# The opening of a Mamba-2 SSD and gated feed-forward kernel: x issued behind B, the first weights fetched by halves, and the masks and fillers moved

## The chip, the cores and the metric

The kernel runs on one core of a Trainium2 chip. The metric is the device time of one execution in microseconds. A core has TensorE (PE for its products, PEld for its weight loads), VectorE (DVE), ScalarE (ACT), GpSimd (POOL) and SyncE (SP); transfers are issued on the queues of SyncE, ScalarE and GpSimd.

## What is computed

A chunked state-space scan (SSD) with 4 batches, 8 heads, 768 positions, head size 32 and state size 16; its result, turned to 3072 tokens of 256 features, goes through a feed-forward with a quick GELU.

```python
def _attn_ref(x, a, B, C):
    log_a = np.log(np.clip(a, 1e-06, 1.0))
    for c in range(nc):                      # chunks of 32 positions
        cum = np.cumsum(la, axis=-1)
        L = np.exp(cum[:, :, :, None] - cum[:, :, None, :]) * causal
        M = np.einsum('bhin,bhjn->bhij', Cc, Bc) * L
        y_intra = np.einsum('bhij,bhjd->bhid', M, xc)
        y_inter = np.einsum('bhin,bhnd->bhid', Cc, state) * np.exp(cum)[:, :, :, None]
        y[:, :, sl] = y_intra + y_inter
        Bx = np.einsum('bhjn,bhjd->bhjnd', Bc, xc) * decay_from_j[:, :, :, None, None]
        state = decay_full[:, :, None, None] * state + np.sum(Bx, axis=2)

def _moe_ref(x, w_in, w_out):                # 3072 x 256, 256 x 2048, 2048 x 256
    h = x @ w_in
    g = h * (1.0 / (1.0 + np.exp(-1.702 * h)))
    return g @ w_out
```

`w_in` and `w_out` arrive as 64-bit floats; the kernel reads them as pairs of 32-bit words and makes fp32 of them on the chip.

## The kernel before

The tokens go in six groups of 512 (`g`): 128 positions of each of the 4 batches. Each group has two pairs (`p`) of batches. For each group the SSD makes `yT`, the feed-forward's input; `hidden` and `project_all` (group 0) or the steps of `first` and `product` (the later groups) are the dense work. Each engine executes its instructions in the order in which the program text emits them: `in_order` at the end ties each instruction to the one before it on its engine. So the place of a call in the text is its place in the engine's queue, and a wait holds all that is behind it on that engine.

The change lies in the opening, the SSD of group 0 before the first dense product, and in its surroundings:

- **Loads.** `a` goes out first on SyncE. C's eight blocks are issued alternately by ScalarE and SyncE, B's eight by GpSimd (five) and SyncE (three), both by `load_blocks` (L130). Behind B, SyncE issues `fetch(0)`, the first piece of w_in, in two transfers (L179). GpSimd makes `pick` and `first`, then issues x of pair 0 (`load`, L146, two transfers); x of pair 1 stands further down, behind `drop_of(0)`.
- **Decays.** ScalarE takes the logarithm of a (L364), VectorE's scan (L368) makes `cum`. On PE, `mask` (L506) and `differ` (L512) make the exponents of both pairs in PSUM, `rows_first` (L501) those of the states; ScalarE's `decay_exp` (L542) makes `L`. Ahead of them PE runs fillers that compute nothing of use: `pads` (L427, 32 x 32 products) and `dense` (L431, wide ones).
- **Scores.** `turn_blocks` (L554) transposes C and B on VectorE. The masked copies of C are made for pair 0 by VectorE (`mask_first`, L578) and for pair 1 by ScalarE (`mask_blocks`, L587). `score` (L610) multiplies, and `weigh` (L621) multiplies the scores into `L` in place. `turn_back` (L568) transposes B back, `ends_first` (L473) scales it.
- **y and state.** `finish` step 0 has `intra` (L735) of pair 0, `gain` (L641) makes the increment of the state out of x and the scaled B, `keep_first` (L657) copies it on ScalarE, `finish` step 1 has `intra` of pair 1, `inter` (L722) and the four copies to `yT` (L747).
- **Weights.** A piece of w_in goes through `fields` (L200, L203), `clamp` (L212, L214, on ScalarE), `rounded` (L219) and `join` (L233, L239). Pieces 0 to 3 hold two of the sixteen column blocks `f` each, pieces 4 and 5 four each. `hidden(0, f)` (L796) needs block `f`, and `narrow` continues the pieces between the `hidden` calls.
- **Tables.** `table(f)` (L313) is a tiny activation that makes ScalarE switch to the function's table: Ln, then Exp, then Silu.
- `fold_ident(k)` (L350) makes two halves of `idents`, which the scans of later pairs read. `held` in `fetch` is a one-column memset on an engine, which makes the transfer wait for that engine's place.

Of the kernel before, what the change touches and what calls it, by code (L numbers as in the profile page):

```python
# [8 lines left out]
FP32 = mybir.dt.float32  # L9
# [26 lines left out]
def kernel(  # L36
# [122 lines left out]
    def fetch(i, queue=nc.sync, held=None):  # L159
        name, f, n = PIECES[i]  # L160
        if n == 2 and f % 4:
            t = pieces.pop(i - 1)[:, 2 * n * DM:]
        else:
            t = pieces[i] = words(f"bits{i}")
            t = t[:, :2 * n * DM]
        if held:
            held.memset(t[:, :1], 0)
# [7 lines left out]
        for k in range(2):  # L175
            if i:
                queue.dma_start(out=dst[k], in_=src[k])
            else:
                queue.dma_start(out=dst[:, :, k].rearrange("k p e -> p k e"),  # L179
                                in_=src[:, :, k].rearrange("k p e -> p k e"))  # L180
# [116 lines left out]
    fetch(0)  # L297
    pick = const.tile([P, NB, Q], FP32, name="pick")
    nc.gpsimd.memset(pick, 1.0)
    for r in range(R):  # L300
        rows = pick[32 * r:32 * r + 32]
        nc.gpsimd.affine_select(out=rows, in_=rows, pattern=[[-NH, NB], [-1, Q]],  # L302
                                compare_op=ALU.is_equal, fill=0.0, base=-Q * r,
                                channel_multiplier=1)
    firsts[0] = ssd.tile([P, NB, P], FP32, tag="first", name="first", bufs=1)
    nc.gpsimd.memset(firsts[0], 0.0)
    load(0, "x", nc.gpsimd)
# [55 lines left out]
    for k in range(2):  # L363
# [5 lines left out]
        out=flat_cum, data0=carry, data1=flat_cum, initial=0.0, op0=ALU.mult, op1=ALU.add)  # L369

# [317 lines left out]
    def finish(pairs, steps=range(2)):  # L688
# [56 lines left out]
        if early:  # L745
# [5 lines left out]
            if 0 in steps:  # L751
                for k in range(2):
                    dense(begun_y["banks"][0][:, 2 * P:])
                intra(0, pairs[0])
                return
            for t in range(NK):
                intra(1, pairs[1], (t,))
                copied(0, t)
# [28 lines left out]
    def hidden(g, f):  # L787
# [4 lines left out]
        for k in range(NK):  # L792
            n = 1 if g or NK * f + k < 5 else 4 if NK * (NF - f) - k <= 12 else 2
# [268 lines left out]
    pads(14, busy)  # L1062
    dense(busy, 3)
# [8 lines left out]
    pads(16, both[:, 0, 2 * P:], False)  # L1072
    differ_of(0)
    turn_blocks(0, "C")
    mask_blocks(1)
    decay_exp(0, None, both[:, :, :2 * Q * H])
    drop_of(0)
    load(1, "x", nc.gpsimd)
    mask_first(0)
# [4 lines left out]
    table(AF.Silu)  # L1084
# [3 lines left out]
    turn_blocks(0, "B")  # L1088
    score(range(PG))
    turn_back()  # L1090
    fold_ident(1)
# [3 lines left out]
    fetch(1, held=nc.vector)  # L1095
    weigh(0, (slice(1, 2),))
    fields(0, (0,), 1)
# [16 lines left out]
    finish(range(PG), (1,))  # L1114
    join(0, 2, (0,))
# [5 lines left out]
    rounded(1)  # L1121
    join(1, 2, (0,))
# [236 lines left out]
```

## Time and profile before

| | |
|---|---|
| median of 3 runs | 349.73 us (348.93 to 352.75) |
| the profiled execution | 349.18 us, of which the span is 347.5 us |
| PE busy | 341.1 us, 98% of the span |
| PEld, VectorE, ScalarE, GpSimd busy | 281.0, 256.2, 150.0, 46.0 us |
| granted TensorE clock (mean) | 1.00 |
| first dense product of group 0 (L796) starts | 17.26 us |
| last of x's transfers for group 0 lands | 14.46 us |

The span runs from the program's first instruction to its last; the 1.68 us around it belong to the execution's time. All times within the profile are counted from the span's start. A row of the timeline gives start, length, engine, line, operation, output and inputs; the bracket is the idle time of that engine ahead of the row and what ended it. "issue" there is idle time for which the profile shows no cause.

### The profile page before, as it was taken

The page shows a single profiled execution, that of the slowest core. Times are in us where ns is not written, and L with a number is a line of the kernel's source. Part 1 is how long each engine was busy: PE and PEld are TensorE (multiplying, and loading weights), DVE is VectorE, ACT ScalarE, POOL GpSimd, SP SyncE. Part 2 cuts the span into 40 slices and gives each one's busy share as a digit, 9 for nine tenths or more (in the row PEclk, how much of TensorE's full clock was granted, in tenths as well). Part 3 has the DMA queues.
Part 4 walks back from the last instruction along what each step waited for, and adds up shares of the span by engine and source line. Part 5 has one row for each costly group of instructions (what it writes and reads, how often), then busy time and mean ns, then how long its engine had stood idle before and what let it go on. Part 6 is the DMA issues. An engine that isn't in the chain of part 4 may idle for free.

```text
span 347.5 us, 8538 instructions
## 1 busy us (share of the span) xinstructions
PE 341.1 (98%) x3514; PEld 281.0 (81%) x3514; DVE 256.2 (74%) x477; ACT 150.0 (43%) x335; POOL 46.0 (13%) x82
## 2 busy tenths in 40 slices
PE   8799999999999999999999999999999999999996
PEld 6668964555788888888888888888888888899996
DVE  7889999999799897839985639985555653555463
ACT  6779664005454314644333543442444322554320
POOL 8305820300495000000000000000000000000000
PEclk9999999999999999999999999999999999999999
DMA  4699995704639000554122345120000120000221
GB/s 129 208 298 281 279 165 125 116 24 76 106 85 135 2 0 17 89 116 89 29 35 61 47 100 100 25 33 6 2 4 0 20 32 12 0 2 0 33 31 60
DMA packets 82831, 25.79 MB, mean 74 GB/s; under 512 B 68856, under 2 KB 81144, under 8 KB 82792
## 3 DMA queue, kind: packets, MB, share of 16 engines
q1 hardware_dynamic: 79912, 23.19, 31.4%
q0 software_dynamic: 1888, 1.74, 2.4%
q8 instruction: 27, 0.44, 0.5%
q10 hardware_dynamic: 992, 0.33, 0.4%
q14 instruction: 12, 0.10, 0.1%
HBM read 21.99 MB, written 3.24 MB: 73 GB/s over the span
## 4 chain that ended last, share of the span: by engine, by line
PE 95%; POOL 2%; DMA 1%; issue 0%; ACT 0%; DVE 0%; POOLq 0%
PE acc L954 28%; PE X L852 19%; PE Y L862 14%; PE h L796 10%; PE o L894 8%; PE acc L961 7%; PE y L735 2%; PE y L722 2%; PE cb L610 2%; PE A L641 1%; DMA x<-in_x_dram 1%; POOL zB L130 1%; POOL x L146 1%; POOL pick L302 0%; ACT S L657 0%
## 5 line engine op out<-in xcount | busy, mean ns | idle before, releaser
L857 ACT ACTIVATE ac<-X 128x256 f32<-128x256 f32 x76 | 29.1, 383 | 79.8 <-PE X L852 79.4
L954 PE MATMUL acc<-mg,mw 128*128 128x256 f32 x192 | 54.5, 379 | 0.0
L981 DVE TENSOR_TENSOR gT<-Y,ac 128x512 f32<-128x512 f32 x38 | 26.2, 690 | 37.1 <-PE Y L862 33.6
L829 ACT ACTIVATE gT<-gT 128x512 f32<-128x512 f32 (+1 forms) x76 | 39.3, 519 | 31.6 <-DVE gT L981 31.0
L852 PE MATMUL X<-my,mi 128*128 128x256 f32 x152 | 45.1, 379 | 0.0
L981 DVE TENSOR_TENSOR gT<-Y,b 128x256 f32<-128x256 f32 x38 | 15.8, 418 | 34.4 <-PE Y L862 34.4
L954 PEld LDWEIGHTS acc<-mg,mw 128*128 128x128 f32 x192 | 36.5, 190 | 5.0
L796 PE MATMUL h<-yT,w_in 128*128 128x128 f32 (+2 forms) x182 | 36.3, 357 | 0.1
L954 PE MATMUL acc<-gT,w_out 128*128 128x256 f32 x128 | 35.5, 379 | 0.0
L796 PEld LDWEIGHTS h<-yT,w_in 128*128 128x128 f32 x182 | 26.8, 191 | 8.3 <-issue 5.6
L852 PEld LDWEIGHTS X<-my,mi 128*128 128x128 f32 x152 | 28.0, 190 | 3.7
L894 PE MATMUL o<-gT,w_out 128*128 128x512 f32 x64 | 28.6, 597 | 0.0
L820 DVE TENSOR_TENSOR mg<-gT 128x512 f32<-128x512 f32 x40 | 27.2, 681 | 0.0
L954 PEld LDWEIGHTS acc<-gT,w_out 128*128 128x128 f32 x128 | 24.2, 190 | 3.4 <-ACT yT L769 0.2
L857 ACT ACTIVATE b<-X 128x256 f32<-128x256 f32 x38 | 14.6, 384 | 20.6 <-PE X L852 20.2
L852 PE MATMUL X<-yT,w_in 128*128 128x256 f32 x76 | 23.2, 389 | 0.0
L862 PE MATMUL Y<-yT,w_in 128*128 128x256 f32 x76 | 22.7, 381 | 0.0
L862 PE MATMUL Y<-my,mi 128*128 128x256 f32 x76 | 22.6, 379 | 0.0
L852 PE MATMUL X<-my,w_in 128*128 128x256 f32 x76 | 22.6, 381 | 0.0
L862 PE MATMUL Y<-yT,mi 128*128 128x256 f32 x76 | 22.5, 379 | 0.0
L894 PEld LDWEIGHTS o<-gT,w_out 128*128 128x128 f32 x64 | 11.8, 190 | 13.2 <-issue 12.4
L1013 POOL DMA_DIRECT2D out_dram<-ob x32 | 17.4, 551 | 26.5 <-DVE ob L1008 26.1
(144 smaller groups left out, 578.9 us busy)
## 6 DMA issues: line engine op xcount, KB each, us to landing
a<-scratch SPq DMA_DIRECT2D x18, 256.0 KB
bits<-in_moe_w_out_dram SPq DMA_DIRECT2D x8, 512.0 KB
x<-in_x_dram SPq DMA_DIRECT2D x20, 128.0 KB
bits<-in_moe_w_in_dram SPq DMA_DIRECT2D x8, 256.0 KB
bits<-in_moe_w_in_dram SPq DMA_DIRECT2D x4, 512.0 KB
out_dram<-ob SPq DMA_DIRECT2D x128, 16.0 KB
af<-in_a_dram SPq DMA_DIRECT2D x20, 64.0 KB
zC<-in_C_dram SPq DMA_DIRECT2D x36, 32.0 KB
```

The source lines that it names most:

```text
L610: nc.tensor.matmul(out=s["cb"][side, r, k].rearrange("p (q i) -> p q i", q=Q), lhsT=BT[rows, k, side], rhs=CT[rows, k, :, side], start=Tru ...
L796: nc.tensor.matmul(out=h[:, cols], lhsT=w_in[:, f, k], rhs=yT[g][:, k, cols], start=(k == 0 and e == 0), stop=(k == NK - 1), skip_group_ch ...
L820: nc.vector.tensor_tensor(out=t[:, 0:2], in0=B[:, :, 1], in1=B[:, 0], op=ALU.subtract)
L829: nc.scalar.activation(o, i, AF.Silu, scale=GELU_SCALE)
L852: nc.tensor.matmul(out=s["X"], lhsT=lhsT, rhs=rhs, start=i == "1", stop=i == "4", skip_group_check=True)
L857: nc.scalar.activation(copy, s["X"], AF.Copy)
L862: nc.tensor.matmul(out=o, lhsT=lhsT, rhs=rhs, start=s.pop("new", False), stop=i != "5", skip_group_check=True)
L894: nc.tensor.matmul(out=o[c], lhsT=w_out[:, c, f], rhs=gT[g, f // 2][:, f % 2], start=(f == 0), stop=(f == NF - 1), skip_group_check=True)
L954: nc.tensor.matmul(out=acc[g][0][i], lhsT=w, rhs=h, start=(j == 0 and (i, 0) in begins), stop=(j == NF // 2 - 1), skip_group_check=True)
L961: nc.tensor.matmul(out=o[k] if type(o) is list else o[:, cols], lhsT=h[:, cols], rhs=w, start=(j == 0 and (i, k) in begins), stop=(j == NF ...
L981: nc.vector.tensor_tensor(out=o, in0=v, in1=w, op=ALU.add)
L1013: (nc.sync if g else nc.gpsimd).dma_start(out=rows[:, b, :, cols], in_=t[32 * r:32 * r + 32, b * P:(b + 1) * P].rearrange("p (u e) -> p u ...
```

## The change

- x of both pairs is issued by GpSimd directly behind B; `pick` and `first` are made later, behind `since_start`.
- `fetch(0)` is split into its two halves (one column block each), held by VectorE: the first behind the scan of `cum`, the second behind C's turn.
- B is turned directly behind C. ScalarE masks C of pair 0, VectorE that of pair 1.
- The switch to the Silu table moves from behind the second exponentials to behind the copies of `finish` step 1.
- `fold_ident(1)` moves from behind `turn_back` to behind `rounded(1)`; the first field operation of piece 0's second half moves between the two `weigh` products of pair 0.
- Fillers: 14 `pads` ahead of the masks become one more `dense`; 16 `pads` ahead of `differ` become 27; one of the two `dense` in `finish` step 0 moves behind the first part of `intra` in step 1. One more product of `hidden(0, 9)` is cut into four instead of two.

```diff
--- before.py
+++ after.py
@@ -156,15 +156,18 @@
     def words(name):
         return wide.tile([P, 2 * PN], U32, tag="bits", name=name, bufs=BUFS)
 
-    def fetch(i, queue=nc.sync, held=None):
+    def fetch(i, queue=nc.sync, held=None, halves=range(2)):
         name, f, n = PIECES[i]
-        if n == 2 and f % 4:
+        if i in pieces:
+            t = pieces[i][:, :2 * n * DM]
+        elif n == 2 and f % 4:
             t = pieces.pop(i - 1)[:, 2 * n * DM:]
         else:
             t = pieces[i] = words(f"bits{i}")
             t = t[:, :2 * n * DM]
         if held:
-            held.memset(t[:, :1], 0)
+            at = 0 if i else 2 * halves[0] * DM
+            held.memset(t[:, at:at + 1], 0)
         if name == "in":
             src = moe_w_in[:, 2 * f * P:2 * (f + n) * P].rearrange("(k p) e -> p k e", p=P)
             dst, src = (v.rearrange(s, h=n, e=2 * P) for v, s in (
@@ -172,7 +175,7 @@
         else:
             src = moe_w_out[f * P:(f + n) * P, :].rearrange("(f p) (h e) -> h p f e", p=P, h=2)
             dst = t.rearrange("p (h f e) -> h p f e", h=2, f=n)
-        for k in range(2):
+        for k in halves:
             if i:
                 queue.dma_start(out=dst[k], in_=src[k])
             else:
@@ -294,17 +297,8 @@
                                 compare_op=ALU.is_ge, fill=-1e5, base=0,
                                 channel_multiplier=-1)
     load_blocks(0, "B", [nc.gpsimd, nc.sync, nc.gpsimd, nc.sync, nc.gpsimd, nc.sync, nc.gpsimd, nc.gpsimd])
-    fetch(0)
-    pick = const.tile([P, NB, Q], FP32, name="pick")
-    nc.gpsimd.memset(pick, 1.0)
-    for r in range(R):
-        rows = pick[32 * r:32 * r + 32]
-        nc.gpsimd.affine_select(out=rows, in_=rows, pattern=[[-NH, NB], [-1, Q]],
-                                compare_op=ALU.is_equal, fill=0.0, base=-Q * r,
-                                channel_multiplier=1)
-    firsts[0] = ssd.tile([P, NB, P], FP32, tag="first", name="first", bufs=1)
-    nc.gpsimd.memset(firsts[0], 0.0)
-    load(0, "x", nc.gpsimd)
+    for p in range(PG):
+        load(p, "x", nc.gpsimd)
     early = const.tile([P, 1], FP32, name="early")
     nc.vector.memset(early, 1.0)
 
@@ -367,6 +361,7 @@
     flat_cum = cum.rearrange("p k s -> p (k s)")
     nc.vector.tensor_tensor_scan(
         out=flat_cum, data0=carry, data1=flat_cum, initial=0.0, op0=ALU.mult, op1=ALU.add)
+    fetch(0, held=nc.vector, halves=(0,))
 
     fans, flat = {}, {}
 
@@ -749,12 +744,13 @@
                     AF.Copy)
 
             if 0 in steps:
-                for k in range(2):
-                    dense(begun_y["banks"][0][:, 2 * P:])
+                dense(begun_y["banks"][0][:, 2 * P:])
                 intra(0, pairs[0])
                 return
             for t in range(NK):
                 intra(1, pairs[1], (t,))
+                if t == 0:
+                    dense(begun_y["banks"][0][:, 2 * P:])
                 copied(0, t)
                 for n, p in enumerate(pairs):
                     inter(n, p, (t,))
@@ -790,7 +786,7 @@
             block(g, j)
         h = bank(f"h{g}_{f}")
         for k in range(NK):
-            n = 1 if g or NK * f + k < 5 else 4 if NK * (NF - f) - k <= 12 else 2
+            n = 1 if g or NK * f + k < 5 else 4 if NK * (NF - f) - k <= 13 else 2
             for e in range(n):
                 cols = slice(e * TG // n, (e + 1) * TG // n)
                 nc.tensor.matmul(out=h[:, cols], lhsT=w_in[:, f, k], rhs=yT[g][:, k, cols],
@@ -1059,8 +1055,8 @@
         differ(p, [(r, ab[p, r]) for r in range(R)])
 
     busy = bank("busy")
-    pads(14, busy)
-    dense(busy, 3)
+    for k in range(2):
+        dense(busy, 3)
     both = area("ab0")
     for r in range(R):
         mask_banks(0, r, both[:, r])
@@ -1069,32 +1065,39 @@
         mask_banks(1, r, seconds[r])
     for r in range(3):
         dense(both[:, r, 2 * P:], 3, False)
-    pads(16, both[:, 0, 2 * P:], False)
+    pads(27, both[:, 0, 2 * P:], False)
     differ_of(0)
     turn_blocks(0, "C")
-    mask_blocks(1)
+    fetch(0, held=nc.vector, halves=(1,))
+    turn_blocks(0, "B")
+    mask_blocks(0)
     decay_exp(0, None, both[:, :, :2 * Q * H])
     drop_of(0)
-    load(1, "x", nc.gpsimd)
-    mask_first(0)
+    mask_first(1)
     differ_of(1)
     rows_first(seconds)
     for r in range(R):
         decay_exp(1, r, seconds[r][:, :3 * P])
-    table(AF.Silu)
     drop_of(1)
     for p in range(PG):
         since_start(p, nc.gpsimd)
-    turn_blocks(0, "B")
+    pick = const.tile([P, NB, Q], FP32, name="pick")
+    nc.gpsimd.memset(pick, 1.0)
+    for r in range(R):
+        rows = pick[32 * r:32 * r + 32]
+        nc.gpsimd.affine_select(out=rows, in_=rows, pattern=[[-NH, NB], [-1, Q]],
+                                compare_op=ALU.is_equal, fill=0.0, base=-Q * r,
+                                channel_multiplier=1)
+    firsts[0] = ssd.tile([P, NB, P], FP32, tag="first", name="first", bufs=1)
+    nc.gpsimd.memset(firsts[0], 0.0)
     score(range(PG))
     turn_back()
-    fold_ident(1)
     fields(0, half=0)
     clamp(0, half=0)
     weigh(0, (slice(0, 1),))
     fetch(1, held=nc.vector)
+    fields(0, (0,), 1)
     weigh(0, (slice(1, 2),))
-    fields(0, (0,), 1)
     clamp(0, half=1)
     for i in range(2, 6):
         fetch(i, held=nc.vector if i == 2 else None)
@@ -1112,6 +1115,7 @@
     gain(range(PG), (0,))
     keep_first(0)
     finish(range(PG), (1,))
+    table(AF.Silu)
     join(0, 2, (0,))
     fields(0, (1,), 1)
     rounded(0, 1)
@@ -1119,6 +1123,7 @@
     fields(1)
     clamp(1)
     rounded(1)
+    fold_ident(1)
     join(1, 2, (0,))
     fields(2)
     clamp(2)
```

## The prediction

> **What bounds the kernel now.** First the page: PE is busy 341.1 of 347.5 us and carries 95% of the chain that ended last, so nearly all that an edit can win lies where PE idles. The busy times by stage put that before 17.3 us (PE busy 3.93 of 5 us in 10:15, 4.50 in 15:20, 5.00 from 20 on, 4.94 in 30:35). So the second view is the chain of waits in order of time:
>
> ```profile
> 7.23 1.77 POOL x L146 x2
> 8.99 0.04 issue
> 9.04 0.27 POOL drops L467
> 9.31 0.85 POOL x L146
> 10.15 4.30 DMA x<-in_x_dram
> 14.46 0.04 issue
> 14.50 0.36 PE y L641 x8
> ...
> 32.09 0.06 issue
> ```
>
> Columns: start, length, what. Ahead of these rows the chain runs on GpSimd through B's issues, `pick` (from 5.14) and `first` (to 7.23); then GpSimd issues x; the last of x's four transfers lands at 14.46; the state increment (L641), its copy (L657, from 14.88), y (L722) and, from 17.33, the dense stage (L796) follow. The last row is the one stop of the dense stage. But the chain names only who was last. Third, the timeline of each engine, for who is second:
>
> ```profile
> 10.28 0.41 PEld L610 LDWEIGHTS cb<-CT,Bt 32*64 32x64 f32 x21 [0.73 <-issue]
> ...
> 11.05 1.29 DVE L621 TENSOR_TENSOR L<-L,cb 128x512 f32<-128x512 f32 x2 [1.39 <-PE cb L610]
> ...
> 10.48 1.28 ACT L313 ACT_TABLE_LOAD   x1
> ...
> 19.16 0.43 DVE L233 SCALAR_TENSOR_TENSOR p<-bits,p 128x256 uint32<-128x256 uint32 x1 [0.75 <-ACT p L214]
> ...
> 25.09 0.69 DVE L200 TENSOR_SCALAR p<-bits 128x1024 uint32<-128x1024 uint32 x1 [0.26 <-DMA bits<-in_moe_w_in_dram]
> ...
> 30.81 1.19 DVE L239 SCALAR_TENSOR_TENSOR w_in<-m,p 128x512 f32<-128x512 f32 x1
> ...
> 32.12 0.94 PEld L796 LDWEIGHTS h<-yT,w_in 128*128 128x128 f32 x5 [0.43 <-ACT p L214]
> ```
>
> Start, length, engine, line, instruction, and in brackets the idle time ahead of it. Three readings. The x wait is only 0.43 us deep on the weight loads of L641. Before it, VectorE waited 1.39 us for the scores, which had stopped 0.73 us inside for nothing that the profile shows. And the last three rows are a second chain, VectorE making w_in out of 64-bit words: it has 0.75 + 0.26 us of slack between 11 and 32 us, and at 32.1 PE waits for it. The row names ScalarE, but the clamp there ended at 31.88; what ended last is w_in, at 30.81 + 1.19 = 32.00. So an earlier start of the dense stage is kept only if the weights come earlier too.
>
> **The change, part by part.**
>
> (a) x straight behind B. Out of x's way go `pick`, `first` (5.14 to 7.23) and `drops` (0.27). The last B issue ends at 5.10, four x issues of 0.90 follow, the last from 7.80. Landing takes 3.1 to 4.3 us (the rows of x), so 10.9 to 12.1. The reader comes to it at about 14.1. The wait goes: 0.43 us. The GpSimd work moved back is wanted first at 32.7 (`X<-az,pick`), and GpSimd idled from 12.1 to 28.9: nothing, and up to 2.1 us of its own time without that cover.
>
> (b) First weights by halves. The SyncE issues move from 5.16 and 5.64 to behind the scan (about 5.97) and behind C's turn (about 7.05). They landed 2.9 and 3.1 us after issue, the last sixteenth of the second 4.7. So 8.9, and 9.9 to 11.7. The first is read at 9.0, under VectorE's wait for the scores: nothing. The second is read between the two `weigh` products at about 11.3: 0 to 0.4, I take 0. Nothing stands behind them on SyncE until the fetch of piece 1. The two memsets are 0.06 each.
>
> (c) B turned behind C, masks swapped. The C mask of 0.69 leaves the place ahead of B's turn. B's transfers are complete only at 7.20 to 7.40 (semaphore updates), with weight packets among them from 6.7; without those perhaps 6.9. The turn starts at 7.1 to 7.3 instead of 7.59, and pair 1's mask ends at about 8.9. But the scores also wait for ScalarE's first exponential (ended 8.75) and PE's own `rows_first` (8.80), against 8.73 for B's turn. Alone this is worth nothing.
>
> (d) PE's fillers. Ahead of the masks 28 small products are swapped for two wide ones (+0.1 us), ahead of `differ` come 54 small ones instead of 32. The 32 took 0.27, so 54 take 0.46. `differ` starts at about 6.2 instead of 5.95, and so do `rows_first`, the second exponentials and the scores: -0.05 to +0.25 late, I take 0.22.
>
> (e) The stop of 0.73 in the scores. The DMA view of 7.8:7.9 has
>
> ```profile
> q1 hardware_dynamic: 31, 0.03, 79.9%
> q8 instruction: 1, 0.02, 59.2%
> ```
>
> one 16 KB instruction packet among the weight packets (948 ns, ended 8.78, 1.5 us before PE went on). The page counts 27 such packets for PE's 7028 rows, one for each 260, so they are taken as PE's own blocks of instructions. If the stop is that packet's lateness, its request at about 6.2 had a crowded 1.6 us; with the weights 0.8 and 1.4 us later it starts around 7.2 and most of the stop goes. Bounds 0 and 0.73; I take 0.57, since the place fits. The Trainium skill (Runtime: NRT & Kernel Launch, Instruction fetch mechanics) has it that the next 16 KiB block is fetched while the present one runs and that crossing is mostly hidden; the trace shows a stop that is not hidden. By the rule the stop has another cause and stays, and the forecast would be 350.1.
>
> (d) and (e) give the scores 0.35 earlier. `weigh`, `ends_first` and the second `weigh` keep their lengths and move by that; the field operation put between the first two only changes places with one behind them.
>
> (f) The second wide filler goes behind part of `intra`: two rows of some 0.25 in the 0.50 that PE waits for S; 0 to 0.1, taken as 0. One more product of f = 9 is cut into four: the stretch of fours takes 10.92/12 = 0.91 us for each 512 columns, the one of twos 5.38/6 = 0.90: nothing.
>
> So the last copy of y ends 0.43 + 0.35 = 0.78 earlier: 16.98 instead of 17.76.
>
> (g) The switch to Silu. Before, it ran from 10.48 to 11.88 with its first use, and ScalarE later idled 1.03 ahead of L657: free. After, it stands behind the last copy and ahead of the clamp of piece 1 (17.66), which had no slack at all: VectorE's 0.75 wait was for it. 1.40 - 0.78 = 0.62 later. The other idents product (0.67) moves into that wait, which is now 1.4 long: nothing, 0.67 without it. From there VectorE is full to 32.0 but for the 0.26 wait on a transfer, whose issue moves 0.35 earlier; I let it take up the 0.26. So w_in for f = 8 comes 0.62 - 0.26 = 0.36 later. PE, 0.78 early, stops some 0.65 at f = 2 and the rest at f = 8, and is 0.36 late. After that it never idles in the windows to 60.
>
> The skill (ScalarE: Activation LUTs, What ACT_TABLE_LOAD costs) adds a drain of 1.38 us to every switch's 1.28. The rows disagree: exponential ended 10.46, load 10.48, next activation 11.77. With it the sum would be 350.9.
>
> **Sum.** The profiled execution took 349.18 (span 347.5 and 1.68 around it); + 0.36 gives 349.5, 0.2 under the median 349.73 of runs that spread from 348.93 to 352.75. A measurement tells about 1% (3.5 us) from no change here, so I forecast no change.
>
> **Rivals.**
>
> Weights keep pace (faster). The stop goes whole and the fillers are free: copies 0.43 + 0.73 = 1.16 earlier, clamp 0.24 late, less 0.26: level. And w_in at 30.81 took 1.19 where its equals take 0.69, while GpSimd clipped `az` from 30.57; if they no longer meet, 0.5 more: 348.7. For: the packet's time. Against: the clip waits for a transfer that moves along.
>
> x is not early enough. x, both weight halves and an instruction packet now share the engines from 7.5 to 11; the last sixteenth of x came 1.3 us behind the other fifteen before. If it still comes at 14.4 the 0.43 is lost: 349.9. Against: two us to spare.
>
> The instruction block (slower). PE enters its next block near 9.9 instead of 10.3 and needs the one behind it at about 13.9. The packet for it started at 12.34; the one after that only at 19.70, 5.1 us after its place was reached at 14.6, when weights held the engines. The fetch of piece 1 is issued 0.6 earlier now. If it gets in front, the block is there 5.1 + 0.9 + 1.5 us after 9.9, at 17.4, PE stands 3.4, and the sum is 349.5 + 3.4 = 352.9. It decides once the packet starts after about 11.6. Against: it has a 2 us lead.
>
> The switch costs what the skill says, a drain after it: 1.4 more in (g) if ScalarE has to empty first, 350.9. Against: the rows at 10.46 to 11.77.
>
> **How the numbers follow.** Forecast 0.50 (own range 348.8 to 350.3); weights keep pace 0.22; x late 0.10; drain 0.08; block 0.10. Predicted is the forecast, 349.5. Lowest: keeping pace with 0.4 of run spread, 348.3. Highest: drain with the 0.4 of (b), 351.3; the block stays outside. Over 1% faster means under 346.2: 0.03, more than all these waits hold. Over 1% slower, above 353.2: 0.06, the worse half of the block. Within: 0.91.
>
> **What would show it.** Right: x issued by 8.8 and no wait for it at L641; scores ending near 10.6; the Silu load directly behind the fourth copy; VectorE's wait ahead of L233 about 1.4 with the idents row before it; PE stopping before f = 2 and near 32.5. Wrong: `h` starting under 16.4 with no such stops (weights keep pace), a PE stop of "issue" over 1 us near 14 (block), an idle ScalarE behind the load (drain), L641 still released by x.

## The result, and the profile after

The changed kernel takes **351.69 us** in the median (350.55 to 353.08, 20 runs), the one before 349.75 (348.87 to 352.75, 20 runs). The ratio is 1.0047, with a 95% interval of 1.0030 to 1.0065: it is slower, by 1.0 to 2.3 us, and outside the forecast range. (The ratios of the experiments below leave out runs over 1.5% above the fastest of their kernel: four of f_held and two of f_x_block.) The profiled execution took 351.75 us, span 350.0, against 349.18 and 347.5.

| us from the span's start | before | after |
|---|---|---|
| full TensorE clock granted from | 4.65 | 5.69 |
| `differ` starts | 5.95 | 6.68 |
| scores end (their stop) | 10.94 (0.49) | 12.45 (1.48) |
| last copy of y ends | 17.76 | 19.03 |
| third write of w_in ends | 20.04 | 22.83 |
| seventh write of w_in (f = 8) ends | 32.01 | 34.57 |
| span | 347.5 | 350.0 |

The last two rows differ by 315.5 and 315.4: here every loss ahead of the seventh write reaches the end at full size.

The chain of waits of the changed kernel, in order of time (start, length, what):

```profile
9.54 0.90 PE cb L605 x46
10.44 1.48 issue
11.91 0.56 PE cb L605 x17
12.57 0.69 DVE L L616
...
18.65 0.38 ACT yT L742
19.05 1.28 ACT L307
20.34 0.20 ACT early L307
20.55 0.62 ACT p L215
21.19 0.73 ACT p L217
21.95 0.44 DVE p L236
```

GpSimd and x are gone from it. In their place stand a stop of 1.48 us in the scores for which the profile has no cause, and behind the last copy the switch to Silu (L307), with the clamp of piece 1 (L215, L217) and VectorE's join (L236) behind it. The timeline of each engine shows who waited (in brackets the idle time ahead of the row, and what ended it):

```profile
9.96 0.29 DVE L203 TENSOR_SCALAR p<-bits 128x256 uint32<-128x256 uint32 x1 [1.24 <-DMA bits<-in_moe_w_in_dram]
...
12.57 0.69 DVE L616 TENSOR_TENSOR L<-L,cb 128x512 f32<-128x512 f32 x1 [2.12 <-PE cb L605]
...
21.95 0.42 DVE L236 SCALAR_TENSOR_TENSOR p<-bits,p 128x256 uint32<-128x256 uint32 x1 [1.19 <-ACT p L217]
...
33.88 0.69 DVE L242 SCALAR_TENSOR_TENSOR w_in<-m,p 128x512 f32<-128x512 f32 x1
```

VectorE's wait for the scores grew from 1.39 to 2.12, its wait for the clamp from 0.75 to 1.19 although the idents product of 0.68 now lies in it, and the first half of the weights is waited for. PE stops at the two places that the prediction named:

```profile
22.98 5.41 PE L792 MATMUL h<-yT,w_in 128*128 128x512 f32 x22 [0.74 <-DVE w_in L242]
...
34.72 1.53 PE L792 MATMUL h<-yT,w_in 128*128 128x256 f32 x6 [0.37 <-DVE w_in L242]
```

**Where the 2.5 us came from**, by the table: the copies end 1.27 later (scores start 0.60 later and take 0.91 longer; from there to the copies 0.24 less, x no longer waited for); from the last copy to the third write it is 3.80 instead of 2.28, so the switch costs 1.52; to the seventh write 0.23 comes back, the wait for a transfer that was 0.26 before. 1.27 + 1.52 - 0.23 = 2.56.

These are two single executions. Before's, 349.18, lies 0.69 under the median of its runs with an undisturbed clock (349.87, next section); the changed kernel's lies 0.13 over its own (351.62). Between these medians the gap is 1.75. The switch and what comes back behind it make 1.52 - 0.23 = 1.29 of that, so some 0.5 us is left for the opening (an estimate from these numbers), not 1.27. The forecast had 0.78 won there.

### The profile page after: what moved, and what is told of

Its sections match the earlier page's. It is cut to its first block, busy times and chain, and to the rows that moved or that the text cites. A ratio compares the mean times of both kernels' runs of the same rounds, so it can differ in the third digit from the quotient of the medians.

```text
span 350.0 us, 8544 instructions
## 1 busy us (share of the span) xinstructions
PE 342.2 (98%) x3514; PEld 281.7 (80%) x3514; DVE 256.4 (73%) x479; ACT 150.0 (43%) x335; POOL 44.3 (13%) x82
## 3 DMA queue, kind: packets, MB, share of 16 engines
q0 software_dynamic: 1888, 1.74, 2.5%
## 4 chain that ended last, share of the span: by engine, by line
PE 93%; DVE 3%; issue 2%; ACT 1%; DVEq 0%
PE acc L950 28%; PE X L848 19%; PE Y L858 14%; PE o L890 8%; PE acc L957 7%; PE h L792 6%; PE y L730 2%; PE cb L605 2%; PE y L717 2%; PE A L636 1%; DVE p L203 1%; DVE p L236 1%; PE ab L507 1%; DVE m L206 1%; PE ab L501 0%
```

## The experiments

Besides the forecast's steps one thing had to be sorted out first. Each run has a mean granted TensorE clock. With a mean of 0.998 to 1.0 the clock stayed full, but for the last microsecond or so of some (in b_cover's profile it falls 1.1 us ahead of the end). Means of 0.993 to 0.995, 0.99 and 0.985 mean that it fell back to half for some 3.4, 6.8 or 10 us, in the profiles at 13 to 25 us, and such runs are longer. Of the kernel before, 156 runs beside the experiments have 99 at the full clock, median 349.87 (348.97 to 352.32), and 57 that fell back, median 352.25. So in the table "full" is the median of the runs with a mean of 0.998 or more, "fell" how many had less. The ratio is to the runs of before on the same chip, those that fell included, with its 95% interval.

| kernel | median (lowest to highest) | full | fell | ratio |
|---|---|---|---|---|
| the changed kernel | 351.69 (350.55 to 353.08) | 351.62 | 2 of 20 | 1.0047 (1.0030 to 1.0065) |
| u_fillers | 351.17 (350.48 to 351.52) | 351.17 | 0 of 12 | 1.0003 (0.9977 to 1.0029) |
| u_table | 350.48 (349.38 to 353.81) | 350.00 | 2 of 12 | 1.0012 (0.9980 to 1.0044) |
| u_fetch | 351.93 (351.10 to 353.03) | 351.93 | 1 of 12 | 1.0037 (1.0013 to 1.0061) |
| u_x | 352.26 (351.24 to 355.39) | 351.45 | 5 of 12 | 1.0063 (1.0029 to 1.0098) |
| v_fill_table | 350.62 (349.37 to 351.81) | 350.62 | 2 of 12 | 0.9997 (0.9975 to 1.0018) |
| f_table | 350.88 (350.38 to 352.01) | 350.80 | 2 of 12 | 1.0005 (0.9981 to 1.0030) |
| f_fill | 350.17 (349.03 to 354.06) | 350.03 | 2 of 12 | 0.9995 (0.9961 to 1.0028) |
| f_x | 350.84 (349.65 to 353.79) | 350.31 | 7 of 12 | 1.0008 (0.9978 to 1.0038) |
| f_halves | 352.41 (349.68 to 353.18) | 349.83 | 9 of 12 | 1.0018 (0.9987 to 1.0049) |
| f_held | 352.54 (349.16 to 356.07) | 349.74 | 10 of 12 | 1.0026 (0.9994 to 1.0058) |
| f_block | 351.78 (348.99 to 353.35) | 349.13 | 9 of 12 | 1.0018 (0.9989 to 1.0047) |
| f_x_block | 353.02 (349.55 to 355.39) | 349.60 | 9 of 12 | 1.0016 (0.9978 to 1.0055) |
| b_warm | 350.83 (350.39 to 351.59) | 350.83 | 0 of 12 | 1.0000 (0.9977 to 1.0024) |
| b_cold | 352.90 (351.38 to 354.31) | none | 12 of 12 | 1.0064 (1.0036 to 1.0091) |
| b_cover | 349.72 (349.35 to 351.67) | 349.72 | 0 of 12 | 0.9987 (0.9965 to 1.0010) |
| g_warm | 355.09 (354.49 to 356.81) | 354.62 | 2 of 6 | 1.0137 (1.0100 to 1.0174) |
| g_cover2 | 350.22 (349.14 to 354.07) | 349.91 | 3 of 12 | 0.9994 (0.9963 to 1.0026) |
| g_cover3 | 350.48 (350.04 to 352.31) | 350.42 | 1 of 12 | 1.0017 (0.9998 to 1.0036) |

Kernels named u_ and v_ undo parts of the change, those named f_ make parts of it (or of a repair) in the kernel before, b_ and g_ are about the clock.

### The switch to Silu

**u_table** is the changed kernel with the switch at its old place, behind the second exponentials:

```diff
     for r in range(R):
         decay_exp(1, r, seconds[r][:, :3 * P])
+    table(AF.Silu)
...
     finish(range(PG), (1,))
-    table(AF.Silu)
```

> The changed kernel with the switch to the Silu table back behind the second exponentials. Theory: the clamp of piece 1 starts right behind the last copy, 1.4 us earlier; w_in for f = 2 comes before PE wants it, the stop of PE at f = 2 (0.74) goes and the one at f = 8 shrinks; 350.3 to 350.9. Rival (the switch was hidden by VectorE's other work, the loss is all in the late scores): less than 0.4 better than the changed kernel, 351.3 or more.

**f_table** is the kernel before with the switch behind the copies and `fold_ident(1)` behind `rounded(1)`:

> The kernel before with the Silu switch alone moved behind the copies of y, and with it the second idents product behind rounded(1). Theory (the switch is the larger part of the loss): the clamp of piece 1 starts 1.40 later than its own place, so the third w_in write ends about 3.8 us after the last copy instead of 2.28, the seventh some 1.2 to 1.5 later than before's 32.0 when the clock comes early, and the lowest time is near 350.1, 1.1 to 1.5 over before's 348.87. Rival (the slack of VectorE hides it): the third write moves by less than 0.4 and the lowest time stays under 349.3.

At the full clock u_table takes 350.00, 1.62 less than the changed kernel, and f_table 350.80, 0.9 more than before's 349.92 in the same job (lowest against lowest 1.26). ScalarE's and VectorE's rows of f_table's timeline show how:

```profile
18.12 1.28 ACT L313 ACT_TABLE_LOAD   x1
19.42 0.20 ACT L313 ACTIVATE early<-early 128x1 f32<-128x1 f32 x1
19.53 0.71 ACT L212 ACTIVATE p<-p,edge 128x512 f32<-128x512 uint32 x1
...
21.02 0.43 DVE L233 SCALAR_TENSOR_TENSOR p<-bits,p 128x256 uint32<-128x256 uint32 x1 [0.51 <-ACT p L214]
```

From load to clamp it is 1.41, and the third write ends at 21.91, 3.80 behind the last copy, as expected. The rival, that VectorE's slack hides it, falls. Over all twenty profiles the third write ends 3.79 to 3.80 behind the last copy in the five kernels with the late switch (the changed kernel, f_table, u_fetch, u_fillers, u_x), and 2.28 to 2.30 in the fourteen others but v_fill_table (2.54). The switch is 0.9 to 1.6 of the 1.75 us between the full-clock medians of the changed kernel and before.

### The fillers and the start of the clock

**u_fillers** gives the changed kernel before's fillers, **f_fill** gives the kernel before the changed one's, **v_fill_table** is the changed kernel with before's fillers and the old place of the switch:

```diff
-    for k in range(2):
-        dense(busy, 3)
+    pads(14, busy)
+    dense(busy, 3)
...
-    pads(27, both[:, 0, 2 * P:], False)
+    pads(16, both[:, 0, 2 * P:], False)
```

(u_fillers; the moved `dense` and the cut in `hidden` go back too.)

> The changed kernel with the fillers of the kernel before (14 pads and one dense ahead of the masks, 16 pads ahead of differ, both dense in finish step 0, the old cut of f = 9). Theory (three separate costs: late fillers, a late instruction packet, the table switch ahead of the clamp): the full clock is granted about 1 us earlier, differ starts near 5.95 instead of 6.68, the packet is asked for that much earlier, the stop in the scores falls from 1.48 to 0.7 or less, the scores end at 10.3 to 11.0 instead of 12.45, and the time is 350.2 to 350.8, about 1.2 us under the changed kernel, still above before by the switch. Rival 1 (the crowd of x and the two weight halves alone makes the loss; the fillers are harmless): the stop stays near 1.5, time within 0.3 of the changed kernel's 351.7. Rival 2 (when the full clock is granted is chance): differ's start bears no relation to the fillers.

> The kernel before with the changed kernel's fillers alone. Theory: the fillers move the place of the stop, from product 43 of the scores to product 47, and little else; the instruction packet starts near 7.8 and takes about 0.95 since x stays out of its way; the moment of the full clock comes by chance, 4.5 to 7.8; the median stays within 0.5 of before, and the seventh w_in write ends at 31.9 to 32.5 with an early clock. Rival (the fillers cost the time, as in the sum's step (d) or more): differ starts at 6.6 or later even with the clock granted near 4.6, and the lowest time is 0.5 or more over before's.

> The changed kernel with both the fillers and the place of the Silu switch of the kernel before; x behind B, the halves, the masks and B's turn stay changed. Theory (fillers and switch are the two losses and add up): copies end near 18.1, w_in's seventh write at 32.1 to 32.3, time within 0.4 of before. Rival (the rest of the change costs by itself through the weight halves that land late): 0.8 or more above before.

The late start of `differ` in the changed kernel's profile was mostly not the fillers. The same six wide fillers (start, length), first in the timeline of before:

```profile
4.28 1.33 PE L431 MATMUL ab<-ones 128*128 128x192 f32 x6
```

and in that of f_table, whose fillers are before's:

```profile
4.28 1.87 PE L431 MATMUL ab<-ones 128*128 128x192 f32 x6
```

The full clock came at 4.65 in the first and at 5.76 in the second; `differ` started at 5.95 and 6.46. Over all profiles of kernels with before's fillers it came anywhere from 4.53 to 7.83, with the changed kernel's from 5.69 to 6.90: the moment is chance. Against f_table, with almost the same clock, the changed kernel's `differ` is 0.22 later (6.68), which is the fillers' share. f_fill is level with before. And u_fillers, whose clock came at 4.53, is the clean comparison with the profile of before: its copies end at 18.09, 0.33 later, its third write 3.8 behind that, its span is 349.1, 1.6 longer.

Two forecasts missed here. u_fillers was to take 350.2 to 350.8 and took 351.17, 0.45 under the changed kernel at the full clock; its stop is 0.77 and its scores end at 11.18. v_fill_table was to be within 0.4 of before and is 0.7 over the 349.90 of before in its job, and 0.6 over u_table, which has the changed fillers: the two losses do not simply add up. Its seventh write (32.66) comes only 0.65 behind that of before, but its span ends 316.4 behind it instead of 315.5; PE has a stop of 0.67 at 73.58, where VectorE is late with a later group.

### The stop in the scores, x and the halves

Counting the products of PE, wherever there is such a stop it stands behind the 223rd of the program, whatever that is: product 43 of the scores with 76 products ahead of `differ`, 47 with 72. In all profiles that stop there PE goes on 1.3 to 1.6 us after the end of the 16 KB instruction packet: 8.78 and 10.28 before, 10.45 and 11.91 after. Of the 1.67 by which that packet ended later, 0.77 is that the 94th product, 130 earlier, came later (6.22, 6.99), 0.48 the way from there to the packet's start (1.61, 2.09), and 0.41 the packet itself (0.95, 1.36).

**u_x** puts `pick`, `first` and x back to their old places, **u_fetch** fetches the first piece whole behind B; **f_x** is before with x behind B alone, **f_halves** with the halves alone, **f_held** with the first piece whole but held until C is turned:

```diff
-    fetch(0)
...
         out=flat_cum, data0=carry, data1=flat_cum, initial=0.0, op0=ALU.mult, op1=ALU.add)
+    fetch(0, held=nc.vector, halves=(0,))
...
     turn_blocks(0, "C")
+    fetch(0, held=nc.vector, halves=(1,))
```

(f_halves.)

> The changed kernel with pick, first and both x loads at their old places on GpSimd. Theory: between 7 and 9 only the weight halves are in the packet's way, it starts near 8 and the stop is about 0.6; but the last of x lands at 14.4 or later and is waited for again; both nearly cancel: 351.0 to 351.6. Rival (early x is the gain that the rest hides): 352.2 or more.

> The changed kernel with the first weights fetched whole by SyncE straight behind B, as before. Theory (the packet waits for whatever is in front of it on its engine): weights move from 6.7 to 8.2 as before, x beside them from 7.5, the packet asked for near 7.0 starts near 8.2 to 8.6 instead of 9.08, the stop is 0.6 to 1.0 instead of 1.48, time 350.9 to 351.4. Rival (halves are a gain, holding the weights back helps): slower than the changed kernel, 352 or more.

> The kernel before with one part of the change alone: x of both pairs issued straight behind B, pick and first made behind since_start. Theory (the span is the end of the seventh write of w_in plus 315.4 us, and that follows from the end of the last copy of y): x lands by 12.5, the wait of 0.43 at L641 goes, the copies end at about 17.3, w_in's seventh write at 31.6, time 0.3 to 0.5 under before; but x now lies beside the weights, and the packet of instructions may be longer on its way, which takes up to 0.4 back. Rival (x behind B is itself the loss, by crowding): 0.5 or more above before.

> The kernel before with the first weights by halves alone, the first held behind the scan, the second behind C's turn; x at its old place. Theory (the halves land late whatever else is on the engines): the first lands near 9 to 10, the second at 11.5 to 12.5, behind the instruction packet; VectorE waits for bits, 0.2 to 1.1 us in all, ahead of or between the two weigh products; the seventh w_in write is 0 to 0.8 later than before's and the time 0 to 0.8 us longer. Rival (it is x beside them that makes them late): the halves land at about 8.9 and 10.5, no wait for bits of over 0.2, the time as before. A packet that takes under 1.1 us would say that it needs x beside it to be slow.

> The kernel before with fetch(0), whole, held by VectorE until behind C's turn. Tells whether the packet of instructions waits behind the first weights. If it does (the prediction's step e), it starts near 7.0 instead of 7.83 and the stop of 0.49 in the scores goes; x still lands last, so the time is level with before or 0.3 better. Rival (the packet takes 1.4 to 1.7 us from its request whatever else moves): it starts at 7.6 to 7.9 as before and the stop stays within 0.2 of 0.49.

| | weights | x | packet's start and length | stop in the scores |
|---|---|---|---|---|
| before | behind B | old place | 7.83, 0.95 | 0.49 |
| f_held | held | old place | 7.58, 1.26 | none |
| f_halves | held by halves | old place | 8.06, 0.96 | none |
| u_x | held by halves | old place | 8.81, 0.98 | 0.45 |
| f_x | behind B | behind B | 9.09, 1.35 | 1.07 |
| u_fetch | behind B | behind B | 9.27, 1.60 | 1.33 |
| u_fillers | held by halves | behind B | 7.82, 1.38 | 0.77 |
| after | held by halves | behind B | 9.08, 1.36 | 1.48 |

Holding the weights back does take the stop away, or nearly, as long as x is not there instead (none, none, 0.45). That is at or below the low end of what the others scatter: with weights behind B and x at its old place six profiles show 0.42 to 1.26 (b_cold 0.42, f_fill 0.44, before 0.49, b_warm 0.75, f_table 0.95, b_cover 1.26). With x behind B the held weights bring nothing: the four such profiles show 0.34 to 1.58 (v_fill_table 0.34, u_fillers 0.77, the changed kernel 1.48, u_table 1.58). So the 0.49 of before is a low one, and the growth to 1.48 is in part a matter of which executions were profiled. That x behind B alone lengthens the stop (f_x 1.07, u_fetch 1.33) can't be told from 0.42 to 1.26. The packet tends to be longer beside x, 1.02 to 1.60 against 0.94 to 1.48, and some of the starts are the clock's: it came at 4.53 in u_fillers and at 7.45 in f_x. What sets the packet's start and length one by one stays open.

Of the forecasts, f_held's holds for the stop and not for the start, 7.58 instead of 7.0, though that is 0.64 behind the 94th product instead of 1.61. Its rival fell with the stop; but there the weights land only at 10.65 and 13.13, and VectorE waits 1.08 and 0.42 for them. u_fetch's missed (stop 1.33 for 0.6 to 1.0, 351.93 for 350.9 to 351.4). u_x's 351.0 to 351.6 holds at the full clock (351.45), without the wait for x that was to come with it: x had landed by 13.74. f_x was to take 0.3 to 0.5 less than before and took 0.4 more (350.31, five runs at the full clock, against 349.90).

The halves themselves are in time alone and late beside x. VectorE's timeline of f_halves, with the first field operation of piece 0 and `weigh`:

```profile
9.09 0.27 DVE L203 TENSOR_SCALAR p<-bits 128x256 uint32<-128x256 uint32 x1
...
11.06 1.29 DVE L624 TENSOR_TENSOR L<-L,cb 128x512 f32<-128x512 f32 x2 [1.50 <-PE cb L613]
```

The field operation waits for nothing. The same rows of u_fillers:

```profile
11.05 0.29 DVE L203 TENSOR_SCALAR p<-bits 128x256 uint32<-128x256 uint32 x1 [2.46 <-DMA bits<-in_moe_w_in_dram]
11.26 0.59 DVE L206 TENSOR_SCALAR m<-bits 128x256 uint32<-128x256 uint32 x1
11.77 0.67 DVE L616 TENSOR_TENSOR L<-L,cb 128x512 f32<-128x512 f32 x1
...
12.50 0.29 DVE L203 TENSOR_SCALAR p<-bits 128x256 uint32<-128x256 uint32 x1
12.71 0.68 DVE L616 TENSOR_TENSOR L<-L,cb 128x512 f32<-128x512 f32 x1
```

In u_fillers the scores are there at 11.2, but `weigh` waits for the fields until 11.77, and the second `weigh` comes 0.94 after it instead of 0.62 (0.21 of that is the field operation that the change put between them). So f_halves bore out the rival written for it. By their semaphores the two halves had landed at 8.60 and 10.92 in f_halves and at 8.46 and 11.38 in u_x, but at 9.9 to 11.0 and 12.5 to 12.6 in the four kernels that hold them by halves with x behind B. In time, x alone and the halves alone show no loss that these runs can tell from none; their clock fell back in 7 and 9 of 12 runs, that of before in 11 and 15 of 35 in the same jobs.

### Moving the place of the stop

**f_block** moves twelve `pads`, 24 products of 32 x 32, from ahead of the masks to `finish` step 0, so that the 224th product falls behind the scores. **f_x_block** does that with x behind B:

```diff
-    pads(14, busy)
+    pads(2, busy)
...
             if 0 in steps:
+                pads(12, begun_y["banks"][0][:, 2 * P:])
```

> The kernel before with 12 of the 14 pads ahead of the masks moved behind the scores (into finish step 0), so that 24 fewer small products stand ahead of the scores and the count behind them is the same. Theory (the stop is at a fixed instruction of PE, the one that begins the third block, reached with product 119 from differ's first and 76 ahead of it): the stop leaves the scores and lies behind their last product; the scores end near 10.2 and weigh starts at 10.3 instead of 11.05; x, still last at 14.4, keeps the time within 0.3 of before. Rival (the stop belongs to the scores themselves): it stays at product 43 of the scores.

> The kernel before with x of both pairs behind B (pick and first made behind since_start) and twelve of the pads ahead of the masks moved into finish step 0, so that the place where PE stops falls behind the scores. Theory: with the stop out of the scores weigh starts at about 10.3 (before 11.05), and with x landed by about 13.3 nothing waits for it: the copies of y end near 16.9 (before 17.76), the seventh w_in write near 31.0 to 31.3, and the lowest time is about 347.9 to 348.3, 0.6 to 1.0 under before's; the median 0.3 to 1.0 under unless the clock falls back oftener. Rival (VectorE's weights set it whatever is won ahead): VectorE is held by bits or by the transfer of piece 1 instead, the seventh write stays near 32.0 and the time within 0.3 of before. Second rival: the stop in turn_back, with x on the engines, grows past 1 us and falls on the path to gain, and the copies end at 17.5 or later.

The weight loads and VectorE's rows of f_block's timeline:

```profile
10.25 1.30 DVE L621 TENSOR_TENSOR L<-L,cb 128x512 f32<-128x512 f32 x2 [0.51 <-PE cb L610]
...
11.00 0.14 PEld L568 LDWEIGHTS b<-ident,Bt 128*128 128x128 f32 x1 [0.62 <-issue]
...
15.46 0.15 PEld L641 LDWEIGHTS y<-x,Be 64*32 64x32 f32 x8 [1.79 <-DMA x<-in_x_dram]
```

The stop moved to the 224th product, now the last of `turn_back`, and `weigh` starts 0.80 earlier. Its full-clock runs, only three, are the lowest group of all (349.13, 0.77 under before's 349.90, where within 0.3 was expected), though x now ends the next wait. That wait is what x behind B should remove; the profiled execution of f_x_block (354.54) ran into the next block instead. PE in its timeline:

```profile
14.61 0.23 PE L633 MATMUL y<-x,Be 64*32 64x64 f32 x2
17.82 0.46 PE L727 MATMUL y<-L,x 64*32 64x64 f32 x31 [2.98 <-issue]
```

and the DMA view of 15.4:15.5, where its packet starts (queue, kind, packets, MB, share of the engines):

```profile
q1 hardware_dynamic: 36, 0.03, 99.4%
q8 instruction: 1, 0.02, 59.5%
```

PE went past its 223rd product at 11.89, 1.2 us after VectorE let `fetch(1)` go (10.69); the packet for the block after started only at 15.41, 3.5 later, among weight packets that kept the engines 99.4% busy, and PE went on 1.45 after its end. The second rival put this stop in `turn_back`, where it was 1.47; the larger one stood one block further on. Not every execution has it: three full-clock runs take 349.60, too little for a stop of 2.98, and still over the forecast 347.9 to 348.3. This is the mechanism of the prediction's slower rival, the instruction block, met in another kernel than the one that it was written for.

### What makes the clock fall back

**b_warm** adds three wide fillers to the kernel before, **b_cold** takes the two of `finish` step 0 away, **b_cover** adds one behind the first part of `intra`, where PE waits 0.50 for S; **g_warm**, **g_cover2** and **g_cover3** put seven, two and three into f_block, under its wait for x:

```diff
             for t in range(NK):
                 intra(1, pairs[1], (t,))
+                if t == 0:
+                    for _ in range(1):
+                        dense(begun_y["banks"][0][:, 2 * P:])
                 copied(0, t)
```

(b_cover.)

> The kernel before with three more wide fillers on PE: one ahead of the last eight products of the state increment (where x is waited for), two behind the first part of intra in step 1 (where S is waited for); 0.25 us each. Theory (the clock falls back after a stretch of 3.4 us in which PE idled too much, between 11 and 18 us): runs with a mean granted clock under 0.998 become rarer, at most 3 of 12 against some 4 of 10 for before; runs at the full clock take 0 to 0.3 us more than before's 349.9. Rival (the fall comes whatever PE does there): the share of such runs stays as before's, 4 to 6 of 12.

> The kernel before without the two wide fillers ahead of intra in finish step 0, so that PE idles 0.5 us more near 11.5 us; all else as before. Theory: the clock falls back oftener than before's 4 of 10, in 7 or more of 12; runs at the full clock take as long as before's, 349.9. Rival (the fall comes whatever PE does there): 3 to 6 of 12.

> f_block (twelve pads moved behind the scores) with seven more wide fillers: six ahead of the last eight products of the state increment, under the wait of 1.63 us for x, one behind the first part of intra in step 1. Theory: f_block's gain stays (runs at the full clock near 349.2, 0.7 under before's 349.9) and the clock falls back in at most 3 of 12 runs instead of 9, so the median is 349.2 to 349.8. Rival 1 (the fall comes whatever PE does): 7 or more of 12 fall back and the median stays near 351.8. Rival 2 (the fillers carry the next instruction block's edge, or end behind x): runs at the full clock take 349.7 or more.

> The kernel before with one more wide filler, 0.5 us, behind the first part of intra in step 1, where PE waits 0.50 us for S. Theory (a filler that lies under a wait costs nothing and keeps the clock up): runs with a mean granted clock under 0.998 in at most 4 of 12, their others at before's 349.9 with at most 0.2 more. Rival (what held in b_warm was the filler ahead of the increment, not this one): 5 or more of 12.

> f_block (twelve pads moved behind the scores) with two more wide fillers, 0.5 us each, ahead of the last eight products of the state increment, under f_block's wait of 1.63 us for x. Theory: runs at the full clock stay at f_block's 349.0 to 349.5, and fewer than its 9 of 12 fall back, 2 to 6; the median is 349.2 to 350.5, under before's. Rival: the fillers end behind x in most executions, runs at the full clock take 349.7 or more.

> As g_cover2 with three such fillers, 1.5 us. Theory: at most 3 of 12 fall back, runs at the full clock take 349.2 to 349.8, the median is 349.3 to 349.9, some 0.2% under before's. Rival: as in g_cover2, 350.0 or more at the full clock.

The busy times by stage (stretch, its length, busy us and instructions of PE, PEld, DVE, ACT, POOL, then granted clock, DMA share, GB/s) of b_cold:

```profile
12.00:15.50 3.50, 1.74 (x101) 1.33 (x102) 3.47 (x10) 2.82 (x8) 0.50 (x2) 1.00 0.73 213
15.50:19.00 3.50, 2.89 (x87) 2.43 (x88) 3.03 (x8) 1.15 (x3) 0.00 (x0) 0.54 0.92 278
19.00:22.50 3.50, 3.50 (x14) 1.79 (x11) 1.17 (x4) 1.72 (x3) 0.00 (x0) 0.50 0.88 260
```

of before:

```profile
12.00:15.50 3.50, 2.37 (x130) 1.60 (x128) 3.47 (x11) 2.40 (x7) 0.07 (x1) 1.00 0.73 228
```

and of b_cover:

```profile
12.00:15.50 3.50, 2.98 (x121) 2.31 (x122) 3.43 (x10) 2.36 (x7) 0.23 (x1) 1.00 0.52 144
```

With PE busy 1.74 of 3.5 us in that stage, all 12 runs of b_cold fall back; with 2.98, none of b_cover's; before, with 2.37 in this profile, falls back in 7 of 23 and 7 of 28 runs of the same two jobs. That the falls come whatever PE does is out. Where the limit lies is open. Counted in stretches of 3.41 us from the moment of the full clock, the nine that end in a fall have PE busy for 0.69 to 2.40 us, but five others, with 1.93 to 2.35 (one of them b_cover's, 2.15 in 8.87:12.28), end in none.

The wide filler takes 0.5 us and not the 0.25 that b_warm's and g_warm's expectations reckoned (two rows each). b_warm's three cost 0.8 at the full clock, and g_warm's seven, 3.5 us under a wait of 1.6, some 5: with them the forecast times failed. Not all of that is the fillers' length. Six and fourteen more products also move the ends of all later instruction blocks, and PE stops for "issue" at 261.17 in b_warm (0.45) and at 207.82 and 262.12 in g_warm (1.11 and 1.35), each time 1.5 us behind the end of a 16 KB packet; before has no such stop there. g_cover2 and g_cover3 fall back less than f_block (3 and 1 of 12, against 9), but at the full clock they no longer keep its 349.13.

**A version that did no worse than either** came out of it: b_cover, one filler under a wait. It takes 349.72 against the 350.22 of before in its job, with no fall in 12 runs; at the full clock it is level with before, and the ratio's interval, 0.9965 to 1.0010, does not exclude 1. It is below the 351.69 of the changed kernel.

## Why the prediction was wrong, point by point

**(e) is the step that failed.** It took 0.57 off the stop (0.73 on the weight loads), because the instruction packet was to start at about 7.2 once the weights were out of its way. It started at 9.08, took 1.36 instead of 0.95, and the stop grew from 0.49 to 1.48 (on the weight loads, where the prediction read it, from 0.73 to 1.72). How far it grew is in part the execution, but in none of the four profiles with held weights and x behind B is it gone: 0.34 to 1.58 is left. f_held, f_halves and u_x (none, none, 0.45) show that the step's premise, held weights let the packet through, holds as long as x keeps its old place; the step left out that (a) puts x's transfers into the same stretch. "x is not early enough" named x, halves and packet on the same engines, but only with x as the one who suffers. The Trainium skill's rule (Runtime: NRT & Kernel Launch, Instruction fetch mechanics), that crossing a block is mostly hidden, is not borne out at this place in most profiles: 0.3 to 1.6 us behind the 223rd product, and 2.98 one block on in f_x_block; f_held and f_halves cross it without a stop.

**(b)** was forecast at nothing, with 0.4 as its worst. The halves landed some 1 us later than reckoned (9.9 and 12.6, for 8.9 and 9.9 to 11.7), as in every profile that has x beside them: the first field operation ran at 9.96 after a wait of 1.24, hidden under the still later scores in the changed kernel, open in u_fillers.

**(d)** 0.22 for the fillers was right at equal clock. The profile shows 0.73; the other 0.5 is the moment of the full clock, which one execution can't tell from a cost. The prediction took before's 4.65 as given.

**(g)** was right in its size, 1.40 forecast and 1.52 measured from copy to write, and in what it would come up against: VectorE held by the clamp, PE stopped before f = 2 and again near 34. The 0.26 at the transfer was absorbed as well (0.23). But its cost was to be paid by 0.78 from (a) and (e); that was the sign of the whole sum. With copies 1.27 late in the two profiles, and some 0.5 by the medians, instead of 0.78 early, nothing paid. The Trainium skill's drain (ScalarE: Activation LUTs, What ACT_TABLE_LOAD costs) is not there: the load ended at 20.33, the activation began at 20.34, so that rival fell.

**(a)** held: x was issued by 8.65, landed by 13.3, and no wait for it is left at the state increment. But its 0.43 (0.27 on the products) was there in one execution and not in each: in four of thirteen profiles with x at its old place (b_cold, b_cover, f_table, u_x) x landed by 13.4 to 13.8 and was not waited for. The prediction took the 14.46 of before as given, as it did the 4.65.

**(c)** shows nothing at its place. **(f)** was taken as 0 and cost 0.24: ScalarE's copy of S ended at 16.55, but the moved filler held PE, and `inter` started 0.38 behind the copy, where in the profile of before it was 0.14. With the 0.22 of (d) that is near the 0.45 between the full-clock medians of the changed kernel and u_fillers. Of *weights keep pace*, one part came true without use: the write for f = 8 took 0.69 instead of 1.19, while a field operation at 31.33 took 1.31 instead.

At the same start of the clock (u_fillers against before) the sum would have been: copies 1.0 early, so +0.14; measured were copies 0.33 late and a span 1.6 longer. The gap of 1.3 is (e) with (b): the stop was 0.77 where next to none was left to it, and `weigh`, waiting for the late first half, started 0.59 behind the scores instead of 0.11. (In the block's rival, 17.4 less 13.9 is 3.5 and not 3.4.)

## What to carry to other kernels

Before a cost is set off against a gain, ask whether the gain rests on the same resource that the change fills: here x took the place on the DMA engines that the weights had left, and the instruction packet gained nothing, while the table switch, moved to the one place where ScalarE had no slack, cost its full 1.5 us. Sort the runs by their mean granted clock before a half per cent is explained, and set one profile's wait against several profiles before it is counted as a gain. A wide filler under a wait can keep the clock up: one in b_cover did, with no cost at the full clock (349.72 against 349.83), though in its profile `inter` too started 0.38 behind the copy of S; with more of them the time was longer (g_cover2 349.91 and g_cover3 350.42 against the 349.13 of f_block's three runs). In these profiles the ends of PE's instruction blocks stand at a fixed count of products; where PE stops at one, small products moved from ahead of it to behind it shift the stop to a place that nobody waits for, if the next block is not then the late one. Products that are added move all later ends too.

## What the runs showed of the hardware

- **The clock.** The full clock came at 4.5 to 7.8 us into the span, by chance. Falls began a whole number of some 3.41 us behind that moment (u_table 6.04 and 12.87; b_cold 5.55 and 15.79; f_block 4.55 and 18.21) and lasted 3.4 or 6.8 us. That agrees with the free-running window of 3413 ns that the Trainium skill gives (TensorE: Matmul & The Clock Gate, Part 1: The HAM clock gate). But PE needs no idle window to fall: in b_cold its longest stop near there was 1.53 us.
- **Instruction packets.** One 16 KB packet took 0.9 to 1.6 us in the opening (2.2 once, in b_warm). The first two started 0.6 to 3.5 us after the block before was entered (0.64 in f_held, 3.52 in f_x_block), the third up to 5.0 us (f_block, 15.83 and 20.88). Where PE stopped, it went on 1.3 to 1.6 us after the packet's end. The last sixteenth of x may be held up by them: it landed 1.0 to 1.9 us behind the end of a packet in nine profiles with x at its old place (before 13.22, 14.46; f_block 14.38, 15.42; f_held 13.50, 15.0). In the other four it was not late, so that the packet is the cause is not shown.
